# A gated pair of linear attention blocks on one core: the folded output weights on quarters of the matmul array, in bursts, regrouped through memory, with 15 kept row tiles

## The chip, the cores and the metric

One Trainium2 chip, one core. The metric is the device time of one execution in microseconds (us). Each kernel was run several times, in rounds with the kernel it is compared with. "Before" is the tuned kernel that the change starts from, "after" the changed one. Where ratios are given they are the mean time of one kernel's runs over that of the other's of the same rounds, so not quite the ratio of the medians that stand beside them. A ratio under 1 is faster.

## The reference, cut to what matters

```python
B, S, D, H = 1, 2048, 640, 32            # 20 columns a head, bf16
def block(x, wqkv, wo):
    q, k, v = heads(x @ wqkv)
    phi = lambda t: where(t > 0, t + 1, exp(t)) + 1e-6
    pq, pk = phi(q), phi(k)
    kv  = einsum("bhsd,bhse->bhde", pk, v);   z = pk summed over s
    o = einsum("bhqd,bhde->bhqe", pq, kv) / (einsum("bhqd,bhd->bhq", pq, z) + 1e-6)
    return o @ wo
g = sigmoid((x * gate_w).sum(-1))
return g * block(x, A_wqkv, A_wo) + (1 - g) * block(x, B_wqkv, B_wo)
```

## The kernel before

Names of the engines: PE is TensorE (PEld its loading of weights), DVE VectorE, ACT ScalarE, POOL GpSimd, SPq the DMA queue that SyncE issues. PSUM is the memory that PE writes, eight banks in this program. Stages, in PE's order: K of both branches (phi of x times Wk), G = phi(K)^T x for A and then B with the Q tiles as filling between, and O. The heads' kv never appears over the sequence: kv = (G Wv) with a mask that keeps the 20x20 blocks, and W' = kv times Wo, so that an output row is (phi(q), scaled by gate over denominator) times W'. The output is the sum of both branches. While W' of B is being made, PE computes A's part of NOA row tiles (`o_part`), which ACT copies to the side and DVE adds later (`o_rest`).

```python
NOA = 13
OA = [XNf[:, 2048 + 1280 * i : 3328 + 1280 * i].bitcast(f32) for i in range(6)]
OA += [PK["B"][:, 1280 * i : 1280 * i + 1280].bitcast(f32) for i in range(7)]

def kv_unit(X):                       # per u of 6: 5 matmuls 128x120 weights, 120 columns
    ...
    r = e.matmul(PS[0:GR, ps.slot, GR*i : GR*i+GR], WV[X][:, c, lo:lo+GR],
                 gv[:, c, :, lo//5 : lo//5+24], start=(c == 0), stop=(c == NC-1))
    ...                               # DVE: times the mask, into KVL

def wp_unit(X, u):                    # GR = 120 rows of W'
    e.matmul(a[0:GR, 0:512], KVL[X][:, u, :], WO[X][:, u, 0:512], start=True, stop=True)
    e.matmul(a[0:GR, 512:D], KVL[X][:, u, :], WO[X][:, u, 512:D], start=True, stop=True)
    ...                               # ACT: 640 columns out of PSUM into WST
    dma("SP", ..., WP[X][lo//5 : hi//5, :, :], WST[X][r:GR, u, :], ...)   # inside the chip

# K stage, for every tile and branch: DVE's two operations
e.tensor_scalar(EK, EK, 1.0, EPS, op0=ALU.min, op1=ALU.add)               # "kt"
e.scalar_tensor_tensor(PKt[X][:, t, :], psw(ps, D), 0.0, EK, op0=ALU.max, op1=ALU.add)  # frees PSUM

# the end of PE's order (kv and W' of A stand earlier, between B's G)
o_part(0); o_part(1); o_part(2); den("B"); o_part(3); kv_unit("B"); o_part(4)
for u in range(NU):
    wp_unit("B", u)
    if u % 2 == 0:
        o_part(5 + u // 2)
for t in range(8, NOA): o_part(t)
...
for t in range(NOA): o_rest(t)
for t in range(NOA, NT - 1): out_unit(t)       # A and B together
out_last(NT - 1)
```

## Time and profile before

| | before |
|---|---|
| time, median of 3 runs | 189.1 us (188.46 to 189.16) |
| profiled span | 187.6 us |
| PE busy | 184.6 us, 98% |
| DVE, ACT busy | 135.4 us (72%), 95.6 us (51%) |
| PE's waits for a compute engine after the start | none |
| W' and kv of both branches on PE | 3.26 and 3.3 us |

How to read it: PE is busy all the time and at its full pace, so a change counts by the PE time that it takes away and by the PE waits that it makes. The page's lines are in the prediction below. One more row of this profile is needed later, DVE's "kt" of the K stage, which takes 0.33 us every time (DVE's order of work, start and duration in us):

```profile
33.38 0.33 DVE L549 TENSOR_SCALAR EK<-EK 128x640 bf16<-128x640 bf16 x1 [0.38 <-ACT EK L546]
```

### The profile page before, as it was taken

Reading aid. Unit: us, or ns where it says so; the run is one execution under the profiler, and the core shown is the slowest. Engines: PE = TensorE matmul, PEld = TensorE weight load, DVE = VectorE, ACT = ScalarE, POOL = GpSimd, SP = SyncE. Lnnn points to the kernel's source line nnn. Section 1 sums busy time; section 2 is a strip of 40 time slices with the busy share of each in tenths; the row PEclk is TensorE's granted clock in tenths of the full one; section 3 lists DMA queues with packets and bytes.
Section 4 is the critical chain, followed back from the end, with each engine's and each line's share of the span. In section 5 each row is a group of like instructions: output and inputs, shape, how many; then the busy total and the mean of one; then the engine's idle time right before and its main releaser. Section 6 shows DMA issues by size and latency. Waiting matters only on the chain.

```text
span 187.6 us, 3202 instructions
## 1 busy us (share of the span) xinstructions
PE 184.6 (98%) x1261; PEld 107.9 (58%) x1261; DVE 135.4 (72%) x260; ACT 95.6 (51%) x171; POOL 0.8 (0%) x8
## 2 busy tenths in 40 slices
PE   8999999999999999999999999999999999999995
PEld 4555555555555656665557556655556655555552
DVE  2388888888833555487798999879996999965600
ACT  5365655556554546544675667877524594100012
POOL 1000000000000000000000000000000000000000
PEclk9999999999999999999999999999999999999999
DMA  7999999996001011011701222540015165132322
GB/s 185 293 163 158 252 392 364 344 214 136 4 0 35 0 38 35 0 35 24 92 10 31 56 49 48 124 116 3 0 35 118 32 153 134 39 140 105 136 79 70
DMA packets 36301, 19.89 MB, mean 106 GB/s; under 512 B 25630, under 2 KB 36286, under 8 KB 36286
## 3 DMA queue, kind: packets, MB, share of 16 engines
q1 hardware_dynamic: 35844, 19.48, 41.6%
q8 instruction: 10, 0.16, 0.4%
q10 hardware_dynamic: 442, 0.20, 0.4%
q14 instruction: 5, 0.04, 0.1%
HBM read 9.39 MB, written 2.62 MB: 64 GB/s over the span
## 4 chain that ended last, share of the span: by engine, by line
PE 96%; DMA 2%; SPq 0%; DVE 0%; issue 0%; DVEq 0%
PE ps L904 23%; PE ps L744 23%; PE ps L513 18%; PE ps L618 18%; PE ps L619 5%; PE ps L514 5%; DMA WKW<-in_A_wqkv_dram 2%; PE ps L660 2%; PE ps L698 1%; SPq L343 0%; PE ps L699 0%; DVE TSB L948 0%; DVEq L230 0%; PE ps L494 0%
## 5 line engine op out<-in xcount | busy, mean ns | idle before, releaser
L513 PE MATMUL ps<-WKW,XT 128*128 128x512 bf16 x160 | 44.4, 381 | 0.3 <-DMA WKW<-in_A_wqkv_dram 0.3
L761 ACT ACTIVATE EK<-ps 128x512 bf16<-128x512 f32 x40 | 23.9, 598 | 31.5 <-PE ps L744 29.4
L514 PE MATMUL ps<-WKW,XT 128*128 128x128 bf16 (+1 forms) x160 | 35.2, 220 | 0.0
L546 ACT ACTIVATE EK<-ps 128x640 bf16<-128x640 f32 x32 | 22.4, 704 | 10.8 <-DVE EK L549 5.9
L513 PEld LDWEIGHTS ps<-WKW,XT 128*128 128x128 bf16 x160 | 15.7, 98 | 19.8 <-DMA WKW<-in_A_wqkv_dram 0.6
L744 PE MATMUL ps<-XT,WQA 128*128 128x512 bf16 x100 | 24.5, 379 | 0.0
L744 PE MATMUL ps<-XT,WQB 128*128 128x512 bf16 x100 | 23.7, 379 | 0.0
L618 PE MATMUL ps<-XN,PKB 128*128 128x512 bf16 x80 | 23.5, 379 | 0.0
L618 PE MATMUL ps<-XN,PKA 128*128 128x512 bf16 x80 | 23.5, 379 | 0.0
L771 DVE TENSOR_SCALAR EK<-EK 128x512 bf16<-128x512 bf16 x40 | 11.6, 291 | 14.9 <-ACT EK L761 14.8
L619 PE MATMUL ps<-XN,PKA 128*128 128x129 bf16 x80 | 17.6, 220 | 0.0
L619 PE MATMUL ps<-XN,PKB 128*128 128x129 bf16 x80 | 17.6, 220 | 0.0
L904 PE MATMUL ps<-WPA,EX 128*128 128x512 bf16 x120 | 17.3, 299 | 0.0
L904 PE MATMUL ps<-WPB,PKA 128*128 128x512 bf16 x120 | 16.5, 299 | 0.0
L744 PEld LDWEIGHTS ps<-XT,WQB 128*128 128x128 bf16 x100 | 10.9, 117 | 8.5
L514 PEld LDWEIGHTS ps<-WKW,XT 128*128 128x128 bf16 x160 | 15.8, 98 | 0.0
L549 DVE TENSOR_SCALAR EK<-EK 128x640 bf16<-128x640 bf16 x32 | 10.4, 326 | 7.1 <-ACT EK L546 7.1
L744 PEld LDWEIGHTS ps<-XT,WQA 128*128 128x128 bf16 x100 | 10.6, 117 | 8.1
L618 PEld LDWEIGHTS ps<-XN,PKA 128*128 128x128 bf16 x80 | 9.4, 118 | 7.9
L618 PEld LDWEIGHTS ps<-XN,PKB 128*128 128x128 bf16 x80 | 9.4, 117 | 7.8
L950 ACT ACTIVATE TSB<-ps 128x640 bf16<-128x640 f32 (+1 forms) x3 | 2.0, 668 | 23.2 <-PE ps L904 23.2
L557 DVE SCALAR_TENSOR_TENSOR PKA<-ps,EK 128x640 bf16<-128x640 f32 x16 | 13.2, 825 | 0.6
(77 smaller groups left out, 239.9 us busy)
## 6 DMA issues: line engine op xcount, KB each, us to landing
out_dram<-TSB SPq DMA_DIRECT2D x15, 160.0 KB, 1.8
XN<-in_A_x_dram SPq DMA_DIRECT2D x1, 2240.0 KB, 9.0
WKW<-in_A_wqkv_dram SPq DMA_DIRECT2D x5, 160.0 KB, 4.2
WKW<-in_B_wqkv_dram SPq DMA_DIRECT2D x5, 160.0 KB, 4.0
WQA<-in_A_wqkv_dram SPq DMA_DIRECT2D x1, 800.0 KB, 10.7
WQB<-in_B_wqkv_dram SPq DMA_DIRECT2D x1, 800.0 KB, 11.9
WVA<-in_A_wqkv_dram SPq DMA_DIRECT2D x1, 800.0 KB, 12.7
WVB<-in_B_wqkv_dram SPq DMA_DIRECT2D x1, 800.0 KB, 14.3
```

What stands on the lines that cost most here:

```text
L513: e.matmul(a[:, 0:512], l, WK[X][:, c, 0:512], start=(c == 0), stop=(c == NC - 1))
L514: return e.matmul(a[:, 512:w], l, WK[X][:, c, 512:w], start=(c == 0), stop=(c == NC - 1))
L546: op("ACT", lambda e: e.activation(EK[:, ek.slot, :], psw(ps, D), ACT.Exp), act_cost(D), ins=[ps] + first, outs=[ek], name="ke")
L549: lambda e: e.tensor_scalar(EK[:, ek.slot, :], EK[:, ek.slot, :], 1.0, EPS, op0=ALU.min, op1=ALU.add),
L557: lambda e: e.scalar_tensor_tensor(PKt[X][:, t, :], psw(ps, D), 0.0, EK[:, ek.slot, :], op0=ALU.max, op1=ALU.add),
L618: e.matmul(a[:, 0:512], l, XN[:, t, 0:512], start=(t == 0), stop=(t == NT - 1))
L619: return e.matmul(a[:, 512 : D + 1], l, XN[:, t, 512 : D + 1], start=(t == 0), stop=(t == NT - 1))
L660: r = e.matmul(PS[0:GR, ps.slot, GR * i : GR * i + GR], WV[X][:, c, lo : lo + GR], gv[:, c, :, lo // 5 : lo // 5 + 24], start=(c == 0), st ...
L744: r = e.matmul(PS[:, ps.slot, :], WQ[X][:, c, g::5], XT[:, c, 512 * b : 512 * b + 512], start=(c == 0), stop=(c == NC - 1),)
L761: lambda e: e.activation(EQ[:, eq.slot, :], PS[:, ps.slot, :], ACT.Exp),
L771: lambda e: e.tensor_scalar(EQ[:, eq.slot, :], EQ[:, eq.slot, :], 1.0, EPS, op0=ALU.min, op1=ALU.add),
L904: r = e.matmul(a[:, l0 - lo : h0 - lo], PQ[X, b][:, g, 128 * (t % 4) : 128 * (t % 4) + 128], WP[X][:, g, l0:h0], start=(X == first and g = ...
```

## The change

Its intent: W' is block diagonal by heads, so blocks of 60 rows fit into a 64x64 quarter of the array, and four of them can stream at once. Each branch gets two bursts (320 columns of W' each), whose results come out of PSUM in four large copies. The order of rows that the quarters leave is mended by five stores to memory and one load. As that way is longer, 15 of A's row tiles are kept instead of 13, to give PE work meanwhile. Rows that the quarters read beyond the blocks must be zero: GpSimd clears four pads. The diff, cut to its core:

```diff
-    WV = {X: sb("WV" + X, [128, NC, D], bf) for X in XS}
-    WO = {X: sb("WO" + X, [GR, NU, D], bf) for X in XS}
+    WV = {X: sb("WV" + X, [128, NC, D + 8], bf) for X in XS}
+    WO = {X: sb("WO" + X, [128, NU, D], bf) for X in XS}
-    NOA = 13
+    NOA = 15
-    OA += [PK["B"][:, 1280 * i : 1280 * i + 1280].bitcast(f32) for i in range(7)]
+    OA += [PK["B"][:, 1280 * i : 1280 * i + 1280].bitcast(f32) for i in range(8)]
+    OA += [XT[:, :, :].rearrange("p c s -> p (c s)")[:, 0:1280].bitcast(f32)]
+    for X in XS:
+        pads += [op("POOL", lambda e, X=X: e.memset(WV[X][:, :, 0:4], 0.0), ...)]
+        pads += [op("POOL", lambda e, X=X: e.memset(WO[X][0:4, 0:5, :], 0.0), ...)]
+    for o in pads:
+        o.deps += bpk["B", 8].writers          # not before B's ninth K tile
...
-    kv: 6 units of 5 matmuls with 120 weights, 120 columns
+    kv: 5 such units with 128 weights, and one of 5 matmuls with 104 weights, 40 columns
-    def wp_unit(X, u): ...
+    def wp_burst(X, half):
+        ps = [Buf("wp", "ps", 2) for _ in range(2)]; lo = HALF * half      # HALF = 320
+            for k in range(3):
+                for a, b in ((0, 192), (192, HALF)) if k == 1 else ((0, HALF),):
+                    for t in range(4 * k, min(4 * k + 4, 11)):
+                        c, r, u = t // 2 % 2, t % 2 if t < 10 else 1, t // 2
+                        x = e.matmul(o[:, HALF*k + a : HALF*k + b],        # o: PSUM rows 64c..
+                                     KVL[X][64*r : 64*r + w, u, d : d + p],
+                                     WO[X][64*r : 64*r + w, u, lo + a : lo + b], start=True, stop=True)
+        ...     # two copies of 960 columns (ACT; for B's last one DVE), after the second
+        ...     # burst five stores to wps in memory and one load of all of it into WP
...
-    o_part(3)
     kv_unit("B")
-    o_part(4)
-    for u in range(NU): wp_unit("B", u) ...
+    o_part(3); o_part(4); wp_burst("B", 0); o_part(5); o_part(6); wp_burst("B", 1); o_part(7)
+    ft_op[2].behind, ft_op[3].behind = last_st[0], last_ld[0]   # order in the DMA queue
```

(`ft_op` are the transposes that turn B's scales; there are four, for four tiles of the sequence each.)

More of the change, by code (lines that the diff above doesn't have):

```diff
@@ L20 @@
 NU = 6
+HR = 60
+HALF = 320
 def _bf16_bits(a):
@@ L30, in _consts @@
     p = np.arange(128)[:, None]
-    bd = (p // 20 == np.arange(24)[None, :] // 4).astype(np.float32)
-    return _bf16_bits(bd)
-CW = 24
+    q, m = p % 64, np.arange(24)[None, :]
+    bd = np.where(p < 64, (q >= 4) & ((q - 4) // 20 == m // 4), (q < 60) & (3 + q // 20 == m // 4))
+    be = q // 20 == m[:, 0:8] // 4
+    return _bf16_bits(np.concatenate([bd, be], axis=1).astype(np.float32))
+CW = 32
 XS_W = 672
@@ L40, with __init__ @@
 class Buf:
-    def __init__(self, name, pool=None, n=1):
-        self.name, self.pool, self.n = name, pool, n
+    def __init__(self, name, pool=None, n=1, at=(0, 2, 4, 6)):
+        self.name, self.pool, self.n, self.at = name, pool, n, at
         self.writers, self.readers = [], []
@@ L107, in can @@
                 w = max(w, d.end + (HOP if d.eng != o.eng or d.dma else 0.0))
+            skip = set()
             for b in o.outs:
                 if b.pool and b.slot is None:
-                    got = self.pick(b, w)
+                    got = self.pick(b, w, skip)
                     if got is None:
@@ L113, in can @@
                     w = max(w, got[0])
+                    skip |= set(range(got[1], got[1] + b.n))
             return w
@@ L144, in run @@
                 at[e] = w + o.dma[0]
-                o.end = max(w + o.dma[0] + 1500.0, bus[0]) + o.dma[1] / o.dma[2]
+                o.end = max(w + o.dma[0] + o.dma[3], bus[0]) + o.dma[1] / o.dma[2]
                 bus[0] = o.end
@@ L163, in run, with pick @@
         return max(o.end for o in self.ops)
-    def pick(self, b, t):
+    def pick(self, b, t, skip=()):
         pool = self.free[b.pool]
@@ L169, in pick @@
         for x in pool:
-            have[x[1]] = x[0]
+            if x[1] not in skip:
+                have[x[1]] = x[0]
         if b.n == 1:
-            if not pool:
+            if not have:
                 return None
@@ L176, in pick @@
             return best[0], best[3]
-        c = [(max(have[s], have[s + 1]), s) for s in have if s % 2 == 0 and s + 1 in have]
+        c = [(max(have[i] for i in range(s, s + b.n)), s) for s in b.at if all(i in have for i in range(s, s + b.n))]
         return min(c) if c else None
@@ L296, in body @@
     GS = {X: sb("GS" + X, [128, NC, D], bf) for X in XS}
-    KVL = {X: sb("KVL" + X, [GR, NU, GR], bf) for X in XS}
-    WST = {X: WKW[0:GR, i * NU * D : (i + 1) * NU * D].rearrange("p (u f) -> p u f", u=NU) for i, X in enumerate(XS)}
+    KVL = {X: sb("KVL" + X, [128, NU, GR], bf) for X in XS}
+    WST = {X: WKW[:, i * NU * D : (i + 1) * NU * D].rearrange("p (u f) -> p u f", u=NU) for i, X in enumerate(XS)}
     WP = {X: sb("WP" + X, [128, NC, D], bf) for X in XS}
@@ L328, in body @@
     IDN = sb("IDN", [128, 128], bf)
-    BDM = CST[0:GR, 0:24]
+    BDM = CST[:, 0:24]
+    BDE = CST[64:104, 24:32]
     sch = Sched({"ps": 8, "ek": NEK, "eq": NEQ, "os": NOS})
@@ L339, in dma @@
     def dma(q, name, dst, src, nbytes, ins=(), outs=(), after=(), issue=450.0, transpose=False, prio=None):
+        timing = (330.0, 1500.0) if not transpose else (140.0, 1500.0) if loading else (1000.0, 1150.0)
         def fn(e):
@@ L343, in fn @@
                 return e.dma_start(d, src() if callable(src) else src, transpose=transpose)
-        o = op(q, fn, 0.0, ins, outs, after, prio=prio, name=name, dma=(issue, nbytes, 95.0 if transpose else 330.0))
+        o = op(q, fn, 0.0, ins, outs, after, prio=prio, name=name, dma=(issue, nbytes) + timing)
         if loading:
@@ L369, in body @@
     bwv = {X: Buf("wv" + X) for X in XS}
-    bwo = {X: Buf("wo" + X) for X in XS}
+    bwo = {}
     op("DVE", lambda e: e.memset(ONE[:, :], 1.0), 120.0, outs=[bone], name="one")
@@ L386, in body @@
     zgw = op("POOL", lambda e: e.memset(GWZ[:, :], 0.0), 200.0, name="zgw")
+    bpad = {X: Buf("pad") for X in XS}
+    pads = []
+    for X in XS:
+        pads += [op("POOL", lambda e, X=X: e.memset(WV[X][:, :, 0:4], 0.0), 100.0, outs=[bpad[X]], prio=10**6, name="wvpad")]
+        pads += [op("POOL", lambda e, X=X: e.memset(WO[X][0:4, 0:5, :], 0.0), 1500.0, outs=[bpad[X]], prio=10**6, name="wopad")]
     bxo = Buf("xo")
@@ L403, in xt_dma @@
             outs=bxt[t0:t1],
-            issue=(t1 - t0) * 850.0,
+            issue=(t1 - t0) * 1250.0,
             transpose=True,
@@ L427, in body @@
     for X in XS:
-        dma("SP", "wv" + X, WV[X][:, :, :], w3(X, 2), 819200, outs=[bwv[X]])
+        dma("SP", "wv" + X, WV[X][:, :, 4 : D + 4], w3(X, 2), 819200, outs=[bwv[X]])
     for X in XS:
-        bo5 = Buf("wo5" + X)
-        dma("SP", "wo" + X, WO[X][:, 0:5, :], wo[X][0:600, :].rearrange("(u p) n -> p u n", p=GR), 768000, outs=[bwo[X]])
-        dma("SP", "wo5" + X, WO[X][:, 5, :], wo[X][520:640, :], 153600, outs=[bo5])
-        bwo[X, 5] = bo5
+        for r in range(2):
+            bwo[X, r] = Buf("wo")
+            dma(
+                "SP",
+                "wo%s%d" % (X, r),
+                WO[X][4 + HR * r : 64 + HR * r, 0:5, :],
+                wo[X][0:600, :].rearrange("(u r p) n -> r p u n", r=2, p=HR)[r],
+                384000,
+                outs=[bwo[X, r]],
+            )
+        bwo[X, 2] = Buf("wo")
+        dma("SP", "wo2" + X, WO[X][64:104, 5, :], wo[X][600:640, :], 51200, outs=[bwo[X, 2]])
     loading.clear()
@@ L633, in g_unit @@
             outs=[z],
+            prio=-1,
             name="zc",
@@ L643, in g_unit @@
             outs=[bgs[X, g]],
-            issue=850.0,
+            issue=1250.0,
             transpose=True,
@@ L652, in kv_unit, with out @@
         gv = GS[X][:, :, :].rearrange("p c (g m) -> p c g m", g=NC)
-        for us in ((0, 1, 2, 3), (4, 5)):
-            ps = Buf("kv", "ps")
-            def fn(e, us=us, ps=ps):
-                for i, u in enumerate(us):
-                    lo = GR * u if u < 5 else D - GR
-                    for c in range(NC):
-                        r = e.matmul(
-                            PS[0:GR, ps.slot, GR * i : GR * i + GR],
-                            WV[X][:, c, lo : lo + GR],
-                            gv[:, c, :, lo // 5 : lo // 5 + 24],
-                            start=(c == 0),
-                            stop=(c == NC - 1),
-                        )
-                return r
-            o = op("PE", fn, 5 * len(us) * mm_cost(GR), ins=[bwv[X]] + [bgs[X, g] for g in range(NC)], outs=[ps], name="kv" + X)
-            if X == "A":
-                kv_op[X].append(o)
+        def out(src, u0, n, w, mask, r0, r1):
             b = Buf("kvl")
             bkvl[X].append(b)
-            n = len(us)
             op(
                 "DVE",
-                lambda e, us=us, ps=ps, n=n: e.tensor_tensor(
-                    out=KVL[X][:, us[0] : us[0] + n, :].rearrange("p u (m g) -> p u g m", g=NC),
-                    in0=PS[0:GR, ps.slot, 0 : GR * n].rearrange("p (u g m) -> p u g m", u=n, g=NC),
-                    in1=BDM.unsqueeze(1).unsqueeze(1).to_broadcast([GR, n, NC, 24]),
+                lambda e: e.tensor_tensor(
+                    out=KVL[X][r0:r1, u0 : u0 + n, 0 : w * NC].rearrange("p u (m g) -> p u g m", g=NC),
+                    in0=src().rearrange("p (u g m) -> p u g m", u=n, g=NC),
+                    in1=mask.unsqueeze(1).unsqueeze(1).to_broadcast([r1 - r0, n, NC, w]),
                     op=ALU.mult,
                 ),
-                dve1(GR * n),
+                dve1(w * NC * n),
                 ins=[ps, bcst],
@@ L688, in kv_unit @@
             )
-    bwp = {}
-    bwpm = {X: [] for X in XS}
-    def wp_unit(X, u):
-        ps = Buf("wp", "ps", 2)
-        def fn(e):
-            a = psw(ps, D)
-            e.matmul(a[0:GR, 0:512], KVL[X][:, u, :], WO[X][:, u, 0:512], start=True, stop=True)
-            return e.matmul(a[0:GR, 512:D], KVL[X][:, u, :], WO[X][:, u, 512:D], start=True, stop=True)
-        op(
-            "PE",
-            fn,
-            mm_cost(512) + mm_cost(128),
-            ins=[bkvl[X][u // 4], bwo[X] if u < 5 else bwo[X, 5]],
-            outs=[ps],
-            name="wp%s%d" % (X, u),
-        )
-        b = Buf("wst")
-        op(
-            "ACT",
-            lambda e: e.activation(WST[X][:, u, :], psw(ps, D)[0:GR, :], ACT.Copy),
-            act_cost(D),
-            ins=[ps],
-            outs=[b],
-            prio=-1,
-            name="wpc",
-        )
-        bwp[X, u] = b
-        d = Buf("wpm")
-        bwpm[X].append(d)
-        r = 80 if u == 5 else 0
-        lo, hi = GR * u, min(D, GR * u + GR)
-        dma(
-            "SP",
-            "wpm%s%d" % (X, u),
-            WP[X][lo // 5 : hi // 5, :, :],
-            WST[X][r:GR, u, :],
-            1280 * (hi - lo),
-            ins=[b],
-            outs=[d],
-            issue=850.0,
@@ new lines, in kv_unit, with fn @@
+        for us in ((0, 1, 2, 3), (4, 5)):
+            ps = Buf("kv", "ps")
+            def fn(e, us=us, ps=ps):
+                for i, u in enumerate(us):
+                    for c in range(NC):
+                        lo, n, w = (GR * u, 128, 24) if u < 5 else (540, 104, 8)
+                        r = e.matmul(
+                            PS[0:n, ps.slot, GR * i : GR * i + NC * w],
+                            WV[X][:, c, lo : lo + n],
+                            gv[:, c, :, 24 * u : 24 * u + w],
+                            start=(c == 0),
+                            stop=(c == NC - 1),
+                        )
+                return r
+            o = op("PE", fn, 5 * len(us) * 55.0, ins=[bwv[X], bpad[X]] + [bgs[X, g] for g in range(NC)], outs=[ps], name="kv" + X)
+            if X == "A":
+                kv_op[X].append(o)
+            n = min(us[-1], 4) - us[0] + 1
+            out(lambda ps=ps, n=n: PS[:, ps.slot, 0 : GR * n], us[0], n, 24, BDM, 0, 128)
+            if 5 in us:
+                out(lambda ps=ps: PS[64:104, ps.slot, GR : GR + 40], 5, 1, 8, BDE, 64, 104)
@@ new lines, in body @@
+    bwst = {(X, r): Buf("wst") for X in XS for r in range(2)}
+    bwps = {X: [] for X in XS}
+    WPD = {X: nc.dram_tensor("wps" + X, [D, D], bf, kind="Internal").ap() for X in XS}
+    bwpm = {X: [Buf("wpm")] for X in XS}
+    def wp_burst(X, half):
+        ps = [Buf("wp", "ps", 2) for _ in range(2)]
+        lo = HALF * half
+        def fn(e):
+            for k in range(3):
+                for a, b in ((0, 192), (192, HALF)) if k == 1 else ((0, HALF),):
+                    for t in range(4 * k, min(4 * k + 4, 11)):
+                        c, r, u = t // 2 % 2, t % 2 if t < 10 else 1, t // 2
+                        w, p = (64 - 4 * r, HR) if t < 10 else (40, 40)
+                        d = HR * r if t < 10 else 0
+                        o = PS[64 * c : 64 * c + p, ps[r].slot : ps[r].slot + 2, :].rearrange("p a b -> p (a b)")
+                        x = e.matmul(
+                            o[:, HALF * k + a : HALF * k + b],
+                            KVL[X][64 * r : 64 * r + w, u, d : d + p],
+                            WO[X][64 * r : 64 * r + w, u, lo + a : lo + b],
+                            start=True,
+                            stop=True,
+                        )
+            return x
+        op("PE", fn, 640.0, ins=bkvl[X] + [bwo[X, i] for i in range(3)] + [bpad[X]], outs=ps, name="wp%s%d" % (X, half))
+        for r in range(2):
+            dst = WST[X][0:124, 3 * r : 3 * r + 3, lo : lo + HALF]
+            src = lambda r=r: psw(ps[r], 3 * HALF)[0:124, :].rearrange("p (k n) -> p k n", k=3)
+            if X == "B" and half and r:
+                op(
+                    "DVE",
+                    lambda e, dst=dst, src=src: e.tensor_copy(dst, src()),
+                    dve1(3 * HALF),
+                    ins=[ps[r]],
+                    outs=[bwst[X, r]],
+                    prio=-1,
+                    name="wpc",
+                )
+            else:
+                op(
+                    "ACT",
+                    lambda e, dst=dst, src=src: e.activation(dst, src(), ACT.Copy),
+                    act_cost(3 * HALF),
+                    ins=[ps[r]],
+                    outs=[bwst[X, r]],
+                    prio=-1 if X == "A" else None,
+                    name="wpc",
+                )
+            if half == 0:
+                continue
+            for c in range(2):
+                st(X, r, c, 3 * r, 2 if c else 3, HR, 120 * c + HR * r)
+            if r:
+                st(X, r, 2, 5, 1, 40, 600)
+        if half == 1:
+            last_ld[0] = dma("SP", "wpl" + X, WP[X][:, :, :], WPD[X].rearrange("(p g) n -> p g n", g=NC), 819200, ins=bwps[X], outs=bwpm[X], prio=-1)
@@ new lines, in body, with st @@
+    last_st, last_ld = [None], [None]
+    def st(X, r, c, slot, n, rows, row):
+        h = 64 * min(c, 1)
+        b = Buf("wps")
+        bwps[X].append(b)
+        last_st[0] = dma(
+            "SP",
+            "wps%s%d%d" % (X, r, c),
+            bass.AP(tensor=WPD[X].tensor, offset=WPD[X].offset + D * row, ap=[[D, rows], [240 * D, n], [1, D]]),
+            WST[X][h : h + rows, slot : slot + n, :],
+            1280 * rows * n,
+            ins=[bwst[X, r]],
+            outs=[b],
+            issue=450.0,
@@ L833, in den @@
                 after=[red_op[b]] if b in red_op else (),
-                issue=900.0,
+                issue=1250.0,
                 transpose=True,
@@ L874, in den @@
                 after=kv_op[X],
-                issue=900.0,
+                issue=1250.0,
                 transpose=True,
@@ L920, in o_mm @@
         )
-    boa = {}
+    boa, adds = {}, {}
     def o_part(t):
@@ L938, in o_post @@
         if eng == "ADD":
-            op(
+            adds[t] = op(
                 "DVE",
@@ L1004, in f @@
             elif g == 2:
+                if k == 1:
+                    wp_burst("A", 0)
                 q_next(1)
-                wp_unit("A", 2 * k)
-                wp_unit("A", 2 * k + 1)
             elif g == 3:
+                if k == 0:
+                    wp_burst("A", 1)
                 q_next(2)
@@ L1022, in body @@
     den("B")
+    kv_unit("B")
     o_part(3)
-    kv_unit("B")
     o_part(4)
-    for u in range(NU):
-        wp_unit("B", u)
-        if u % 2 == 0:
-            o_part(5 + u // 2)
+    wp_burst("B", 0)
+    o_part(5)
+    o_part(6)
+    wp_burst("B", 1)
+    o_part(7)
     for t in range(8, NOA):
         o_part(t)
+    ft_op[2].behind, ft_op[3].behind = last_st[0], last_ld[0]
     for b in range(3):
@@ L1041, in body @@
     out_last(NT - 1)
+    for h in range(2):
+        pqs_op["B", 3, h].behind = adds[3 + h]
     span = sch.run()
```

## The prediction

> **What bounds the kernel now.** I read the busy shares first, then the slices, then the chain that ended last, then TensorE's rows with shapes kept apart, and last the order of work from 138 us on.
>
> The page of the kernel before, parts 1, 2 and 4:
>
> ```profile
> PE 184.6 (98%) x1261; PEld 107.9 (58%) x1261; DVE 135.4 (72%) x260; ACT 95.6 (51%) x171; POOL 0.8 (0%) x8
> ...
> PE   8999999999999999999999999999999999999995
> ...
> DVE  2388888888833555487798999879996999965600
> ...
> PE 96%; DMA 2%; SPq 0%; DVE 0%; issue 0%; DVEq 0%
> ```
>
> TensorE (PE) has no slice under nine tenths between the first and the last, and the chain that ended last is 96% PE. A busy PE need not be at its peak, so I checked the pace in the order of work: starts of matmuls are 0.27 us apart for every pair of 512 and 128 columns, 0.216 us for a 512, so about 0.42 ns a column, and 0.055 us for a 128. All stages count up to that pace: K 160 pairs, G 160, O 160, each 43.5 us; Q 200 x 0.217 = 43.3; W' and the step before it (called kv here: V's weights times G) 3.3 us each; warm-up and x^T about 4. Together 184.4 us of the span of 187.6. The rest is about 1 us at the head and 2 at the tail. So the kernel is bound by the columns that PE streams. Only work taken from PE, or a new wait of PE, moves the time; DVE and ACT only count where they make PE wait.
>
> PE's rows for the parts that change (line, shapes, count, busy us and mean ns; these means contain about 165 ns of pipeline latency and are not the pace):
>
> ```profile
> L698 PE MATMUL ps<-WOB,KVLB 120*120 120x512 bf16 x6 | 2.1, 380 | 0.0
> L698 PE MATMUL ps<-WOA,KVLA 120*120 120x512 bf16 x6 | 2.0, 379 | 0.0
> ...
> L660 PE MATMUL ps<-GSA,WVA 128*120 128x120 bf16 x30 | 1.8, 218 | 0.0
> L660 PE MATMUL ps<-GSB,WVB 128*120 128x120 bf16 x30 | 1.8, 218 | 0.0
> ```
>
> The order of PE's work around W' of branch B (start us, us, engine, line, operation):
>
> ```profile
> 143.99 1.81 PE L660 MATMUL ps<-GSB,WVB 128*120 128x120 bf16 x30
> 145.64 1.52 PE L904 MATMUL ps<-WPA,EX 128*128 128x512 bf16 x10
> 147.00 0.38 PE L698 MATMUL ps<-WOB,KVLB 120*120 120x512 bf16 x1
> 147.22 0.22 PE L699 MATMUL ps<-WOB,KVLB 120*120 120x128 bf16 x1
> 147.27 1.52 PE L904 MATMUL ps<-WPA,EX 128*128 128x512 bf16 x10
> ...
> 152.44 0.38 PE L698 MATMUL ps<-WOB,KVLB 120*120 120x512 bf16 x1
> 152.66 0.22 PE L699 MATMUL ps<-WOB,KVLB 120*120 120x128 bf16 x1
> 152.72 5.60 PE L904 MATMUL ps<-WPA,EX 128*128 128x512 bf16 x40
> 158.15 1.52 PE L904 MATMUL ps<-WPA,PKA 128*128 128x512 bf16 x10
> 159.51 0.71 PE L904 MATMUL ps<-WPB,PKA 128*128 128x512 bf16 x4
> ```
>
> A unit of W' takes 147.00 to 147.27, i.e. 0.272 us, so six take 1.63 us a branch and twelve 3.26 us. Row tiles of A (L904, WPA; 1.357 us each) fill PE while B's W' is evicted, moved and landed. The last of the six moves is issued at about 155.4 (the DMA queue's moves of WPB run 153.84 to 156.17), would land some 2 us later, and the first use is at 159.51: about 2 us of slack.
>
> **What the Trainium skill says.** (1) "TensorEngine Tiling (Array Packing)", Key Properties: tiles run weight loads and matmuls independently, and changing the tiling mode drains TensorE. No run here shows either: the kernel before uses no quarters. (2) "TensorE: Matmul & The Clock Gate", Measured speedup vs the span model: a pack of tiles takes one matmul's time plus about 4 ns for each further tile. Not in this trace either; I use it as the best case. (3) "DMA: Bandwidth & Descriptors", Anatomy of one DMA: about 2.0 us fixed, plus bytes at 436 GB/s. It is given for another issuing path; the trace's stores of 160 KB to memory land in 1.8 us, which is near. (4) "SBUF — State Buffer", SBUF: two separate sides: a GpSimd operation and a two-port DVE operation lock each other out for a whole instruction. In this trace GpSimd works only in the first microsecond, so it shows nothing of that.
>
> **The change part by part.**
>
> *W' on quarters.* Removed: 24 matmuls, 3.26 us at pace. Added: per branch two bursts of 15 matmuls of 60 or 40 columns of weights: four tiles at 320 columns, the same four kinds at 192 and at 128 (a bank's border lies between), three at 320. If the tiles of a group run together, a burst streams 136 + 82 + 55 + 136 = 0.41 us (at 0.42 ns a column and 2 ns each). If nothing overlaps it is 11 x 320 x 0.42 ns + fixed parts = 1.5 us. To the best case I add 12 ns x 4 for the packs and two drains; as a drain I take the latency of about 165 ns less what overlaps, an estimate of 0.1 us. That is 0.64 us a burst, 2.56 us for four: **0.7 us less** than 3.26. Should each weight load and matmul keep the pitch of kv (0.055 us a pair), 15 give 0.83 us and nothing is gained.
>
> *kv.* 30 matmuls a branch at 0.055 (143.99 to 145.64) become 25 of the same pitch (120 columns) and 5 of 40 columns, perhaps 0.035: **0.1 to 0.2 us less** over both branches.
>
> *Masks, DVE.* The two multiplications of kv take 1.50 (480 columns) and 0.91 us (240) now; 480, 120 and 40 columns will take 1.5 + 0.55 + 0.3. No more in sum. PE does two A tiles (2.7 us) between kv and the first burst, before one; the first mask starts before kv ends, so I expect no wait.
>
> *Evictions.* Per branch six of 640 columns on ACT (0.70 each) become four of 960: 0.70 + 320 x 0.83 ns = 0.97 each, for B one on DVE (0.82 + 0.33 = 1.15). ACT has room.
>
> *15 tiles instead of 13.* The number of matmuls of O is the same. Two evictions move from the end to the middle and two additions of 0.82 go to DVE, which at 1.36 us a tile has room (it waits for PE 0.5 us before each addition now). The last tile, and so the tail of 2 us, is as before. Gain by itself: none. What it buys is time for the longer way of B's W'.
>
> *The way through memory.* Before: six moves inside the chip. Now five stores to memory, a wait for all, and one load of 0.82 MB. With everything on the clock of the trace: G ends at 138.56; three A tiles to 142.63; kv to 144.2; two tiles to 146.9; burst one to 147.6; two tiles to 150.3; burst two to **150.9**; eight tiles to **161.8**, where PE wants W' of B. From the end of burst two: eviction 1.2 to 2.3 us (0.97 or 1.15, the hop, and up to 0.9 for what ACT or DVE is in the midst of); five stores at 0.4 to 0.77 us of issue each (the moves of before cost 0.77), overlapping the second eviction, about 2.5 to 3; 1.8 from the last issue to landing, less its own issue; the load 2 us fixed + 0.82 MB at the 330 to 390 GB/s of the fullest slices, 4.1 to 4.5 us. In sum about 10 us (8.7 to 12) against 10.9. Expected wait of PE, weighing these ends: **0.3 us**. For A the same way has from about 122 to 138 us: hidden.
>
> *Banks.* A burst wants four of eight PSUM banks at once, beside G's two. ACT evicts a Q tile 1.1 to 1.3 us after its end, about the time of the four G steps between (1.09), so I add **0.1 to 0.2 us** for both bursts of A.
>
> Sum: 189.1 - 0.7 - 0.15 + 0.3 + 0.15 = 188.6; as the first term could well be larger than my drain allows (best case -1.4) I settle on **188.4 us**.
>
> **Rivals.** (a) *The quarters do not overlap, or are bound by issue.* Then bursts cost 0.83 to 1.5 us: the W' term is 0 to +2.7 us, and the time 189 to 191.5. Against it: the skill's packing numbers; for it: nothing in the trace shows any packing. (b) *B's W' comes late.* The way is serial in four pieces, shares the queue with B's transposes (1.2 us of issue each), and has 0.9 us of slack. Each microsecond late is a microsecond of PE: 189 to 190.5. For it: loads of 800 KB took 10.7 us to land, but these were queued behind others. (c) *GpSimd's zeroing of the padding rows holds DVE up in the K stage.* The memset of 128x128 took 0.205 us and of 128x1 0.10, so 3200 elements would take about 2.6 us, twice. DVE works 1.15 us per 1.36 us of PE there. If it is locked out that long, PE could wait 0.5 to 2 us: up to 190. Against it: it is placed where x and the weights have long landed and PSUM gives PE more than a tile of lead. (d) *The bursts run ideally and nothing waits:* 4 x 0.36 us less and kv: 187.5.
>
> **Range and chances.** PE gives at most about 1.6 us, and the losses that I can name, each less likely than not, add to 1 to 2.5. So the predicted time is 188.4 us, with 187.0 to 190.3 as the range for 8 times in 10. Faster by over 2% is under 185.3, more than all of W' could give: 0.02. Slower by over 2% is above 192.9, which needs two rivals at once: 0.03. Within 2%: 0.95.
>
> **What would show it.** In the profile after: the span from the first to the last matmul of a burst near 0.5 to 0.65 us, with the starts of four tiles nearly together (0.8 or more: rival a). PE's waits: none, or a short one at the first WPB matmul on the DMA into WPB (over 0.7 us: rival b). GpSimd rows of some microseconds and DVE's TENSOR_SCALAR of the K stage longer than 326 ns beside them (rival c). DVE's additions 15 in number, the tail of 2 us unchanged. The prediction is wrong if PE's total outside W' and kv changes, or if PE waits in a place not named here.

## The result

| | before | after |
|---|---|---|
| time, median of 6 runs each | 188.94 us (188.46 to 189.25) | 189.44 us (189.21 to 190.12) |
| ratio to before | | 1.0032 (95%: 1.0011 to 1.0054) |
| profiled span | 187.6 us | 188.1 us |

The change is a little slower, though well within 2%. The page of the kernel after, parts 1, 2 and 4:

```profile
PE 183.5 (98%) x1297; PEld 106.4 (57%) x1297; DVE 141.2 (75%) x265; ACT 94.4 (50%) x166; POOL 6.6 (4%) x12
...
PE   9899999979999999999999999999999999999995
...
POOL 1000002900000000000000000000000000000000
...
PE 90%; SPq 3%; DVE 3%; DMA 2%; issue 1%; ACT 0%; DVEq 0%; ACTq 0%
```

PE is busy 1.1 us less, but the span is longer. There is a hole in PE's row in the ninth slice (37 to 42 us), far from anything that W' touches, and GpSimd (POOL) is busy in the two slices just ahead. DVE has come into the chain that ended last with 3%. PE's waits (line, waited for, us in total, times, longest):

```profile
PE ps L537 <- DVE PKA L581: 1.2, 1, 1.2
PE ps L537 <- DMA WKW<-in_A_wqkv_dram: 0.8, 1, 0.8
PE ps L468 <- DVE ONE L383: 0.4, 1, 0.4
```

The last two belong to the head. The first is new: K matmuls (L537) wait for DVE to free PSUM. GpSimd's and DVE's order of work there:

```profile
31.82 2.91 POOL L402 MEMSET WOA<- 4x3200 bf16 x1
...
34.73 2.90 POOL L402 MEMSET WOB<- 4x3200 bf16 x1
```

```profile
33.25 1.67 DVE L573 TENSOR_SCALAR EK<-EK 128x640 bf16<-128x640 bf16 x1 [0.38 <-ACT EK L570]
34.95 0.82 DVE L581 SCALAR_TENSOR_TENSOR PKB<-ps,EK 128x640 bf16<-128x640 f32 x1
35.69 2.13 DVE L573 TENSOR_SCALAR EK<-EK 128x640 bf16<-128x640 bf16 x1
37.85 0.82 DVE L581 SCALAR_TENSOR_TENSOR PKA<-ps,EK 128x640 bf16<-128x640 f32 x1
```

In GpSimd's lines the two short memsets are left out. Two "kt" took 1.67 and 2.13 us instead of 0.33. Each ended 0.19 us after one of the long memsets (34.92 against 34.73, 37.82 against 37.63). DVE's other operation, with one input from PSUM, took its 0.82 us beside the second memset all the same. The changed parts themselves, in PE's order of work:

```profile
143.40 1.69 PE L706 MATMUL ps<-GSB,WVB 128*128 128x120 bf16 x30
144.93 2.88 PE L969 MATMUL ps<-WPA,EX 128*128 128x512 bf16 x20
147.74 0.60 PE L741 MATMUL ps<-WOB,KVLB 64*60 64x320 bf16 x15
148.28 2.89 PE L969 MATMUL ps<-WPA,EX 128*128 128x512 bf16 x20
...
158.44 4.24 PE L969 MATMUL ps<-WPA,PKA 128*128 128x512 bf16 x30
162.76 2.55 PE L969 MATMUL ps<-WPB,PKA 128*128 128x512 bf16 x17
```

kv takes 1.53 us (143.40 to 144.93) instead of 1.65. A burst with what it costs its neighbours takes 0.64 us: two tiles of A are 2.71 us, so 144.93 + 2.71 = 147.64 would be the next start without it, and the work after it starts at 148.28. Three tiles from 158.44 end at 162.51, and the first tile of B starts at 162.76: a wait of some 0.2 us for W'.

For an account that leaves the noisy head out I cut PE's time at the starts of four matmuls of each trace: the 81st of K (at about 16 us), the first of G, the first of A's tiles, and the last of all.

| PE's stretch (us) | before | after | difference |
|---|---|---|---|
| rest of K, to G's first | 32.65 | 33.98 | +1.33 |
| G and Q with A's kv and W' | 90.05 | 89.62 | -0.43 |
| from A's first tile to the last matmul | 46.70 | 46.47 | -0.23 |

The middle row is what both bursts and kv of A save: 1.63 - 2 x 0.66 = 0.31, and 0.12. (By starts of matmuls a burst of A costs 0.63 and the Q matmuls just after it 0.03 more.) The last row is the same for B (0.47 less) with the wait for W' in it. The first row is the padding. Together +0.67; the head happened to be shorter in this trace.

### The profile page after: what moved, and what is told of

Same layout as the page of the kernel before. It is cut to its first block, busy times and chain, and to the rows that moved or that the text cites. A ratio compares the mean times of both kernels' runs of the same rounds, so it can differ in the third digit from the quotient of the medians.

```text
span 188.1 us, 3273 instructions
## 1 busy us (share of the span) xinstructions
PE 183.5 (98%) x1297; PEld 106.4 (57%) x1297; DVE 141.2 (75%) x265; ACT 94.4 (50%) x166; POOL 6.6 (4%) x12
## 4 chain that ended last, share of the span: by engine, by line
PE 90%; SPq 3%; DVE 3%; DMA 2%; issue 1%; ACT 0%; DVEq 0%; ACTq 0%
PE ps L969 23%; PE ps L809 23%; PE ps L644 18%; PE ps L537 14%; PE ps L645 5%; PE ps L538 4%; SPq L354 3%; DMA WKW<-in_B_wqkv_dram 2%; DVE EK L573 2%; PE ps L706 2%; PE ps L741 1%; DVE PKA L581 0%; DVE PKB L581 0%; ACT EK L570 0%; DVE TSB L1013 0%
## 5 line engine op out<-in xcount | busy, mean ns | idle before, releaser
L537 PE MATMUL ps<-WKW,XT 128*128 128x512 bf16 x160 | 44.1, 379 | 2.0 <-DVE PKA L581 1.2
L537 PEld LDWEIGHTS ps<-WKW,XT 128*128 128x128 bf16 x160 | 15.7, 98 | 21.5 <-issue 1.5
L573 DVE TENSOR_SCALAR EK<-EK 128x640 bf16<-128x640 bf16 x32 | 13.5, 422 | 6.8 <-ACT EK L570 6.8
L581 DVE SCALAR_TENSOR_TENSOR PKB<-ps,EK 128x640 bf16<-128x640 f32 x16 | 13.2, 825 | 0.6
```

The costliest lines, as they stand in the source:

```text
L537: e.matmul(a[:, 0:512], l, WK[X][:, c, 0:512], start=(c == 0), stop=(c == NC - 1))
L573: lambda e: e.tensor_scalar(EK[:, ek.slot, :], EK[:, ek.slot, :], 1.0, EPS, op0=ALU.min, op1=ALU.add),
L581: lambda e: e.scalar_tensor_tensor(PKt[X][:, t, :], psw(ps, D), 0.0, EK[:, ek.slot, :], op0=ALU.max, op1=ALU.add),
```

## The experiments

**e1: the pads at the start.** GpSimd clears the pads in the first microseconds. The order of instructions on every engine is the same as in the kernel after.

```diff
     for o in pads:
-        o.deps += bpk["B", 8].writers
+        pass
```

> The changed kernel with one dependency taken away: GpSimd zeroes the four padding blocks in the first microseconds instead of after the ninth K tile of B. Nothing else moves (the order of instructions on every engine is the same). Theory (GpSimd's two memsets of 2.9 us lock DVE's min/add of the K stage out, which holds PSUM banks and so PE): the two long TENSOR_SCALAR of 1.67 and 2.13 us go back to 0.33, PE's wait of 1.2 us on DVE goes, the time falls by 1.2 us to about 188.2, ratio to the kernel before 0.996. Rival (the loss is in the W' of B that goes through memory, or in the bursts): PE's wait may go but the time stays at 189.4, or PE waits elsewhere.

Measured: 188.55 us against 189.02, ratio 0.9970 (0.9958 to 0.9982). All "kt" of the middle of K are 0.33 us again, the rest of K takes 32.65 us as before, and no wait on DVE is left but that of the warm-up. What is left of PE's waits outside the head is the one on the load of W':

```profile
33.62 0.33 DVE L573 TENSOR_SCALAR EK<-EK 128x640 bf16<-128x640 bf16 x1 [0.38 <-ACT EK L570]
```

```profile
PE ps L969 <- DMA WPB<-wpsB: 0.2, 1, 0.2
```

By starts of matmuls this pause is 0.36 us: the wait is counted from the end of the last record only, and a record of 512 columns (0.38 us) is some 0.16 longer than the pace (0.216). So the loss is the pads' place, and without it the change gains 0.3%.

**e2: the pads alone, in the kernel before.** The same four memsets at the same place, into rows of GS that are overwritten later.

```diff
+        pads += [op("POOL", lambda e, X=X: e.memset(GS[X][:, 0, 0:20], 0.0), ...)]
+        pads += [op("POOL", lambda e, X=X: e.memset(GS[X][0:4, :, :], 0.0), ...)]
+    for o in pads:
+        o.deps += bpk["B", 8].writers
```

> The kernel before with only the four memsets added, of the same sizes and at the same place, into rows that are overwritten later; no quarters, no way through memory. Theory: two TENSOR_SCALAR of the K stage become 1.7 and 2.1 us, PE waits about 1.2 us, time 190.1 to 190.2, ratio 1.006. Rival (what delays DVE comes from another part of the change): no effect, ratio 1.000.

Measured: 190.66 us against 189.02, ratio 1.0084 (1.0071 to 1.0097), a little more than expected. The rest of K takes 34.27 us, 1.62 more; every other stretch is as before within 0.01. DVE's order of work and PE's wait:

```profile
33.62 1.81 DVE L554 TENSOR_SCALAR EK<-EK 128x640 bf16<-128x640 bf16 x1 [0.38 <-ACT EK L551]
...
36.21 2.27 DVE L554 TENSOR_SCALAR EK<-EK 128x640 bf16<-128x640 bf16 x1
```

```profile
PE ps L518 <- DVE PKA L562: 1.5, 1, 1.5
```

The memsets cost this much with nothing else of the change present.

**e3: each long memset in ten pieces,** at the place where the change has it.

```diff
-        pads += [op("POOL", lambda e, X=X: e.memset(WO[X][0:4, 0:5, :], 0.0), ...)]
+        for u in range(5):
+            for h in range(2):
+                pads += [op("POOL", lambda e, X=X, u=u, h=h: e.memset(WO[X][0:4, u, 320*h : 320*h+320], 0.0), ...)]
```

> The changed kernel with each memset of 4x3200 cut into ten of 4x320 at the same place, the same bytes in all. If the lock is held for one whole instruction and goes to DVE between two: a memset is about 0.35 us, so no TENSOR_SCALAR should last over 0.7 us, PE does not wait, and the time is that of the early pads, about 188.2 (0.996). Rival (GpSimd keeps the port as long as it has work, or shares it): the TENSOR_SCALAR are delayed by some 5 us in sum as before, and the time is 189.4.

Measured: 188.68 us against 189.02, ratio 0.9978 (0.9966 to 0.9990); rest of K 32.65 us, no wait of PE on DVE. GpSimd worked even longer in sum (row of A's pieces: busy us, mean ns), and the longest "kt" of that stretch took 0.57 us:

```profile
L404 POOL MEMSET WOA<- 4x320 bf16 x10 | 3.6, 405 | 0.0
```

```profile
37.70 0.57 DVE L575 TENSOR_SCALAR EK<-EK 128x640 bf16<-128x640 bf16 x1
```

All 32 "kt" together lost 0.4 us (10.8 us busy against 10.4 before), where they lost 3.1 in the kernel after (13.5). So it is the length of one instruction that counts: DVE gets its turn between two of them, and PE's lead in PSUM covers what delay is left.

**e4: the matmuls of a burst quarter by quarter** (with the early pads).

```diff
-            for k in range(3):
-                for a, b in ...:
-                    for t in range(4 * k, min(4 * k + 4, 11)):
+            for q in ((0, 4, 8), (1, 5, 9, 10), (2, 6), (3, 7)):
+                for t in q:
+                    k = t // 4
+                    for a, b in ...:
```

> As the early pads, but the 15 matmuls of a burst are reordered so that those of one quarter come after another; the same matmuls, banks and evictions (the piece of 192 and of 128 columns of a tile follow each other). Theory (the bursts are short because tiles of four different quarters stream together): nothing overlaps but at the three changes of quarter, a burst takes 1.2 to 1.5 us instead of 0.65, four of them 2.2 to 3.4 us more, ratio to the kernel before 1.008 to 1.014. Rival (the hardware overlaps quarters whatever the order within its queue, or bursts are bound by weight loads and issue): a burst stays below 0.8 us, ratio 0.996 to 0.998.

Measured: 188.64 us against 189.02, ratio 0.9990 (0.9972 to 1.0007). My expectation fell: a burst takes 0.01 us more than in e1 and no more. (The ratio is less good than e1's, but not through the bursts: in this trace PE paused 0.50 us for W' of B.) (Tile 10 belongs to the last quarter and stood in the second's list by my mistake, which made the following record possible.) The first 0.1 us of A's first burst, by forms of matmuls:

```profile
L742 PE MATMUL ps<-WOA,KVLA x4: 310/318/318, 115.9 to 116.0; 64*60 64x320 bf16 x2, 60*60 60x320 bf16 x1, 40*40 40x320 bf16 x1
```

In the program the 40x40 matmul is the ninth of the burst, after four of the first quarter and four of the second. Its record starts 26 ns after the first. So matmuls of different quarters do not keep to the program's order among each other; each quarter worked through its own, and all four began within 30 ns. The order that the change writes is not what makes the overlap.

**e5: 13 kept tiles** (with the early pads).

```diff
-    NOA = 15
+    NOA = 13
```

> The early pads with 13 tiles of A kept instead of 15. Theory (the two extra tiles only fill PE's time while B's W' goes through memory, which takes some 11 us after the second burst): PE waits for the DMA into WPB 2 x 1.36 us longer than the 0.2 us that it waits with 15, so 2.9 us in one wait, and the time is 2.7 us above the early pads: about 191.2, ratio to the kernel before 1.011. Rival (the load would also come sooner, or the two tiles gain something by themselves): a wait under 2 us and a ratio under 1.008, or a loss over 1.015.

Measured: 192.62 us against 188.70, ratio 1.0208 (1.0195 to 1.0222). More than either side expected. PE's wait is about what I had worked out:

```profile
PE ps L969 <- DMA WPB<-wpsB: 3.0, 1, 3.0
```

From A's first tile to the last matmul it is 51.02 us against 46.58 in e1, 4.44 more. The longer wait accounts for 2.8 of it. The rest is PE's clock, which fell after the wait (stretch and its length, busy us of PE, PEld, DVE, ACT and POOL with instructions, granted clock, DMA share, GB/s):

```profile
160.00:165.00 5.00, 3.59 (x15) 1.81 (x16) 0.73 (x1) 0.00 (x0) 0.00 (x0) 0.66 0.27 55
165.00:175.00 10.00, 10.00 (x77) 5.63 (x75) 7.15 (x10) 0.00 (x0) 0.00 (x0) 1.00 0.32 115
```

For some 3 us after the wait a pair of 512 and 128 columns took about twice its time (0.53 us instead of 0.27). The shorter pause of e9 below, 1.3 us, left the clock at 1.00. The quarters and the way through memory without the two extra tiles would have lost about 2%.

**e6: 15 tiles in the kernel before,** and nothing else.

```diff
-    NOA = 13
+    NOA = 15
```

> The kernel before with only the number of kept tiles raised from 13 to 15 (the last in the room of x^T). Theory (number of matmuls and tail unchanged, PE does not wait now): ratio 1.000, within 0.999 to 1.001, and no new wait of PE. Rival (the two evictions or DVE's two more additions cost something, or an output earlier by two tiles gains at the end): a difference over 0.15%.

Measured: 189.07 us against 188.70, ratio 1.0015 (1.0003 to 1.0027). PE has no new wait and its stretches are those of before to 0.01 us (32.65, 90.05, 46.70). The ratio is just outside what I had allowed. As PE's stretches agree and the head changes from trace to trace (last section), I take this as no effect, but a loss of 0.1% outside PE is not excluded.

**e7: B's second burst one tile sooner** (with the early pads).

```diff
-    o_part(6)
     wp_burst("B", 1)
+    o_part(6)
```

> The early pads with B's second burst one row tile of A earlier. Theory (PE's wait of 0.2 to 0.3 us on the DMA into WPB is the whole of what the way through memory costs): the wait goes, 0.2 to 0.3 us less than the early pads, ratio to the kernel before 0.995 to 0.996. Rival (the second burst then waits for PSUM banks or for ACT's eviction of the tile before): a wait before the burst that gives the gain back, ratio as the early pads.

Measured: 188.40 us against 188.70, ratio 0.9985 (0.9973 to 0.9997). PE's wait did not go, it became 0.4 us. The DMA queue's order of work (issue times), and DVE's copy of half of the second burst:

```profile
147.61 3.50 SPq L354 DMA_TRANSPOSE XN<-FF  x2
151.70 2.76 SPq L354 DMA_DIRECT2D wpsB<-WKW  x5
154.51 1.19 SPq L354 DMA_TRANSPOSE XN<-FF  x1
157.05 0.35 SPq L354 DMA_DIRECT2D WPB<-wpsB  x1
```

```profile
150.52 1.16 DVE L757 CAST WKW<-ps 124x960 bf16<-124x960 f32 x1
```

In e1 the stores began at 151.84 and the load at 157.34. A burst that ended 1.3 us earlier moved the load by 0.3 us only, and the load then took 5.0 us to land instead of 4.4. The burst alone does not set the time of the load: here a store of DVE's half stood first in the queue, and DVE's copy ended at 151.68, just before the stores began. How far the pause of PE differs between traces of one plan must be kept in mind: by starts of matmuls it is 0.24 us in the kernel after, 0.36 in e1, 0.12 in e3 and 0.50 in e4, which all order this way alike. The 0.57 here is not clearly more.

**e8: every burst twice** (with the early pads).

```diff
-            for k in range(3):
+            for k in (0, 1, 2, 0, 1, 2):
```

> The early pads with the 15 matmuls of every burst issued twice in a row (the second pass overwrites the same results). Theory (a burst is 0.43 us of streaming in four quarters, from the starts 0, 158, 241, 297 ns and 136 for the last, and 0.2 us for entering and leaving the quarters): each second pass costs 0.43 to 0.45 us, four of them 1.75 us; time 190.3, ratio 1.0065. Rivals: if entering and leaving belong to the matmuls and not to the change of mode, 0.65 each, 2.6 us, ratio 1.011; if the quarters' work were hidden by something else, under 1 us.

Measured: 189.55 us against 188.70, ratio 1.0046 (1.0033 to 1.0059), so 0.0076 above e1 (0.0095 expected). G and Q with two doubled bursts take 90.45 us against 89.62, so 0.415 us for each second pass; the stretch from A's first tile also grew by 0.83. B's first burst and what follows it:

```profile
147.12 1.02 PE L741 MATMUL ps<-WOB,KVLB 64*60 64x320 bf16 x30
148.07 2.89 PE L969 MATMUL ps<-WPA,EX 128*128 128x512 bf16 x20
```

So of a burst's 0.64 to 0.66 us 0.415 is what a further pass costs, that is streaming, and some 0.23 comes once a burst however long it is. I take that as entering and leaving the quarters; no run splits it further.

**e9: the burst sooner, and one more transpose behind the stores** (with the early pads).

```diff
-    ft_op[2].behind, ft_op[3].behind = last_st[0], last_ld[0]
+    ft_op[1].behind, ft_op[2].behind, ft_op[3].behind = last_st[0], last_st[0], last_ld[0]
```

> The early pads, B's second burst one tile sooner, and in the DMA queue the second of the transposes of B's scales behind the stores instead of before them. In the run with only the burst sooner the stores still began at 151.7 us, 0.9 us after ACT's eviction of the second burst had ended, since that transpose stood before them in the queue. Theory (the queue's order, not the burst, set when the load starts): the stores begin right after ACT's eviction, the load lands about a microsecond sooner than in that run, PE's wait on the DMA into WPB (0.2 to 0.4 us) goes, and from PE's first tile of A to its first of B it takes 0.2 us less than with the early pads alone; ratio to the kernel before 0.995 to 0.997, the best of all. Rival (the last store's landing of 2.7 us and the transposes that now run beside the load cost as much): the wait stays, ratio 0.997 to 0.9985.

Measured: 189.00 us against 188.76, ratio 1.0017 (0.9995 to 1.0040). My theory fell, and with it the reading it came from. PE waits 1.1 us for the load, which took 5.6 us from the start of its issue to landing (the issue alone 1.17 instead of 0.35) with two transposes issued just ahead of it. The stores began at 151.00, right after DVE's copy of the second burst (149.81 to 150.97) and not after ACT's (to 150.13): with the burst sooner, the plan puts a store of DVE's half first in the queue. That was so in e7 already, where the transposes had been issued by 151.11 and the stores began at 151.70 with the end of DVE's copy. Counted from A's first tile the stores begin at 13.28 us in both runs, so moving the transpose did not move them; the earlier time here is a shorter head. The profiled execution, 189.92 us, is one of two near 189.9 (the other four took 188.6 to 189.0), and 0.9 us of it has nothing to do with W': its last output took 2.5 us to land instead of 1.6.

**e10: the last two transposes later** (the early pads alone besides; the burst at the change's place). They wait for DVE's additions of the O stage.

```diff
+    for b in (2, 3):
+        ft_op[b].deps.append(adds[b - 2])
```

> The early pads with the last two transposes of B's scales made to wait for DVE's first and second addition of the O stage, so that the load of B's W' has the DMA engines to itself (in the three runs with a transpose just before or beside it the load took 4.4, 5.0 and 5.6 us from issue to landing, the longer the more transposes were in flight, and PE waited 0.2, 0.4 and 1.1 us). Theory (PE's wait is set by what shares the DMA engines with the load): the load lands in under 4 us, PE's wait on the DMA into WPB goes, from PE's first kv of B to its first tile of B it takes 19.2 us instead of 19.5; ratio to the kernel before 0.995 to 0.9975. Rival (the load takes 4.4 us by itself, or the late scales make PE wait at the ninth tile of B): a wait of PE stays or a new one comes, ratio 0.997 or more.

Measured: 187.93 us against 188.89, ratio 0.9947 (0.9934 to 0.9960): the fastest of all, and faster than both kernels. No wait of PE on W' is left, and from A's first tile to the last matmul it takes 46.23 us, 0.35 less than in e1: the whole of e1's pause. The DMA queue:

```profile
151.83 2.94 SPq L354 DMA_DIRECT2D wpsB<-WKW  x5
156.84 0.35 SPq L354 DMA_DIRECT2D WPB<-wpsB  x1
163.96 1.20 SPq L354 DMA_TRANSPOSE XN<-FF  x1
```

One part of the expectation failed: the load still takes 4.3 us by itself (4.3 to 4.7 in the traces with the change's order). Nor does the number of transposes order the loads of e1 and e7 (4.4 and 5.0 us), which had the same ones about them. What moved is its issue, from 157.34 in e1 to 156.84, with no transpose beside the stores that it waits for. It lands at about 161.1, 0.4 us before PE wants it (161.55).

## Why the prediction was right, point by point

- **The time.** 188.4 with 187.0 to 190.3; measured 189.44. In the range, and "within 2%" had 0.95. But the centre was a microsecond low and on the wrong side of the kernel before; that the range held is owed to its width, which rival (c) was counted into, and not to the sum.
- **What bounds the kernel.** Right. All that was found is PE time and waits of PE; the additions on DVE and the copies on ACT never showed.
- **W' on quarters, 0.64 us a burst.** Right in sum: 0.64 to 0.66, and 0.31 to 0.35 us less for a branch. Its parts are near too: 0.41 predicted for streaming, 0.415 measured in e8; 0.05 for packs and 0.2 for two drains, some 0.23 left over (the prediction's parts add to 0.66, not 0.64). How the rest divides was a guess that no run tests. Rival (a), no overlap, is excluded by that (by its own terms it would have reached about 191.8, not 191.5); e4 shows in addition that the overlap does not need the order in which the change writes the matmuls.
- **kv, 0.1 to 0.2 us less over both.** 0.12 us for each branch, 0.24 together.
- **Masks, copies, banks.** The 0.1 to 0.2 us for banks did not show: G and Q shrank by 0.43, all that bursts and kv of A can give.
- **15 tiles gain nothing by themselves.** PE's stretches in e6 say so. What they buy was underrated: with 13, e5 lost not only 2.8 us of waiting but 1.6 more through the clock.
- **The way through memory.** A wait of 0.3 us expected, some 0.2 measured. The way after burst two was estimated at 10 us and took 11: from 151.6 to 162.6, when the load landed (issued at 158.19, 4.4 us). Rival (b) is real, but as small as the sum had it; in e10 it went when the transposes beside the stores and the load were moved away, in e9 it grew to 1.3 us by starts with two transposes just ahead of the load, and an earlier burst alone (e7) did not shorten it.
- **The step that failed is the sum itself:** rival (c) was named with a cost of 0.5 to 2 us and then entered with nothing. GpSimd's memsets were estimated at 2.6 us each and took 2.9, they did hold DVE's "kt" until they ended, as e2 and e3 show, and PE lost 1.33 us (1.62 where they are alone, e2). The counter-argument, that PSUM gives PE more than a tile of lead, was not worked out; DVE lost 1.34 and 1.80 us in two operations just behind each other, 3.1 in sum, and PE's lead covered 1.8 of it. The sum is also 188.7 and not 188.6 (189.1 - 0.7 - 0.15 + 0.3 + 0.15). So it said 0.4 us under the kernel before; with the 1.33 it would have said 0.9 over. Measured in stretches is 0.67 over, as the banks cost nothing (0.15) and kv saved 0.09 more. Without the pads' place, e1, 0.5 us under the kernel before, is what the sum described. The signs that the prediction listed for rival (c), GpSimd rows of some microseconds with long TENSOR_SCALAR beside them, are the ones that the profile shows.

## What to carry to other kernels

When PE is the bound at full pace, a change of one stage is worth what it takes from PE and no more; look for what it loses in quite another stage, where some helper of it (here a memset of four rows) was put because "nothing happens there". An instruction on GpSimd that is off every path can still hold DVE, and its length in one piece counts, not its work: cut it up, or put it where DVE does nothing. A way through memory costs nothing as long as PE has work for it, and what else lies in the DMA queue at that moment is worth more attention than starting it earlier (in e10, 0.35 us).

## What the Trainium skill lacked or had wrong

- "TensorE: Matmul & The Clock Gate", The mechanism (Part 3), says that matmuls start and end strictly in program order. In e4 the ninth matmul of a burst started 26 ns after the first, ahead of six that stand before it: among quarters the order is not kept. The same page's span model (4 ns a further tile) agrees: the four first matmuls of a burst in e1 started at 0, 3, 6 and 10 ns.
- "TensorEngine Tiling (Array Packing)", Key Properties, names the drain at a change of mode without a size: here a burst cost some 0.23 us beside the 0.415 in which its 15 matmuls streamed. No run splits this into the drain and anything else.
- "SBUF — State Buffer", SBUF: two separate sides, is right about the lock for a whole instruction: "kt" of 0.33 us took up to 2.27 beside a memset. What no page has is how long a GpSimd memset runs: 2.75 to 2.9 us for 3200 elements a row on four partitions, 0.405 for 320, but 0.205 for 128 elements on 128 partitions, so the length of the row decided and not the number of rows. Ten pieces of 320 cost PE nothing.
- "DMA: Bandwidth & Descriptors", Anatomy of one DMA, gives its sum for another issuing path. For stores of 160 KB it makes 2.4 us (an estimate from that page), where the outputs took 1.8; the stores of 60 partitions (150 and 225 KB) took 2.6 to 3.2. No page has what a transpose costs a plain transfer beside it: the load of 0.82 MB took 4.3 us with nothing beside it (e10), 4.3 to 4.7 with one on either side, and 5.6 with two issued ahead of it (e9).
- Not a fault of a page, but it limits what such runs can tell: the head, from the first K matmul to the 81st, took between 11.7 and 12.6 us in these traces. In some of them the first few matmuls have records of 0.63 us (512 columns, 0.38 later), in others PE pauses for weights (0.8 us in the kernel after). A difference of 0.2% between two kernels needs the stretches of the trace, not the time alone.
